# Zero rows behind each expert's last row: eight plain stores on SyncE in place of sixteen indirect scatters on GpSimd

## The chip, the cores and the metric

The kernel runs on one core of one Trainium2 chip. The metric is device time in microseconds (us). Of the kernel before, three runs are shown: 447.7, 451.47 and 451.76 us, median 451.47 us. Times inside the text are those of one profiled execution, counted from the start of its span.

## What is computed

A retention layer (a linear attention with a decaying state) over 4 batches, 8 heads, 768 steps and head size 64 gives 3072 token rows of 512 numbers. Those rows go through a mixture of 8 experts, of which each token takes one:

```python
logits = x @ w_gate + modality_bias[modality_id]
e_idx = np.argmax(logits, axis=1)
...
for e in range(E):
    mask = e_idx == e
    ...
    h = np.maximum(x[mask] @ w1[e], 0.0)          # 512 x 1024
    out[mask] = gate_w[mask, None] * (h @ w2[e])  # 1024 x 512
```

## The kernel before, in words

**Rows on the way.** Token rows are made 128 at a time (24 chunks, three of them a group). As soon as a group's experts are known, `scatter` (L410) writes its rows with indirect DMAs on POOL into a DRAM tensor, `x_dram`, that has room for 3072 rows for each expert; a row's place is its expert's base plus its rank in that expert. A row is 514 numbers (2056 bytes): 512 values, the token's number, the gate.

**Jobs.** The expert work is cut into jobs of one slot each: 256 rows of one expert. There are ten jobs "e", two after each of five groups (`EVENTS`), which take slots that are already full, and two jobs "s" at the end, which take the largest of what is left. Counted from 0, the e jobs are 0 to 9, the s jobs 10 and 11. What is left over goes in units of 32 rows (`unit`, two of them written out, the rest in a loop at the end). A unit or an s job can read past an expert's last row; rows of zeros with token number 3072, which the final scatter drops, must stand there.

**A job on the engines** (`run_job`, 16 steps t = 0 to 15). Steps 0 to 7 are `first_slot` (`h_e`, L763), steps 8 to 15 `second` (`o_e`, L778), all in fp32 pieces. PE's order is the order of the code. In job k the next job's inputs are fetched: at t = 2 SP issues four loads of the first weights (`raw`, L703, skipped when the expert is the same as the job's before), at t = 8 `rows_in` issues two loads of 128 rows each from `x_dram` (`xg_e`, `load_rows`, L729) and then the second weights, and at t = 12 `flip_x` puts eight transposes of those rows into PE's stream (`xp_e`, L748), in the middle of job k's own `o_e` matmuls. Places and experts come from lists in SBUF; SP reads each number into a register (`TENSOR_LOAD`, `reg`, L873).

**The queue of SP** is in the code's order too. SP holds one DMA until its waits are met, and everything behind it holds with it. Its DMAs count on eight semaphores in turn, DMAHW0 to DMAHW7, and each first waits for the last DMA on its own semaphore.

**The rows of zeros before.** Behind the last group's routing, `route` puts pieces into a list `todo` that one tick at every odd step works off: `final_m`, `final_b` (which writes the list `lst_f`, L689), `pad_a`, `pad_b`, and then eight times `pad_c`. These fall into job 7 and after. `pad_a` counts the rows of each expert (a matmul into `tot`, L424) and works out on DVE, over all partitions, two places for each partition and expert; `pad_b` ends that, and `pad_c(e)` issues two indirect DMAs on POOL (L470) that write a tile of zeros `zer2` to rows behind expert e's last one up to the slot's end. Places out of range are dropped. All sixteen are in the group `x_rows` with the scatters and the e jobs' row loads: no member of it waits for another. In POOL's queue they stand among the indirect stores of results (`out_dram`, L791), whose row numbers lie in the tiles `xg`.

Of the kernel before, what the change touches and what calls it, by code (L numbers as in the profile page):

```python
# [7 lines left out]
F32 = mybir.dt.float32  # L8
F32R = mybir.dt.float32r
BF16 = mybir.dt.bfloat16  # L10
I32 = mybir.dt.int32
AF = mybir.ActivationFunctionType
ALU = mybir.AluOpType
AX = mybir.AxisListType

P = 128
# [9 lines left out]
NCAND = NE * SPE  # L26
NSLOT = NT // SLOT


EVENTS = {1: -1, 2: 1, 4: -1, 5: 1, 6: -1}  # L30
NEV = 2
# [3 lines left out]
NTAIL = 2  # L35
NUNIT = 144
DENSE = 9
EMPTY = 2 * NCAND
ZROW = NE * NT

ROW = DM + 2
XW = P + 2 * NE
# [8 lines left out]
def kernel(  # L51
# [94 lines left out]
    def setup_b(modi):  # L146
        nc.vector.tensor_tensor(upper, mask, ident, op=ALU.subtract)
        modf = cp.tile([P, NN], F32, name="modf")
        nc.vector.tensor_copy(modf, modi[:, :, 0])
        modn = cp.tile([P, NN], F32, name="modn")  # L150
        nc.vector.tensor_scalar(modn, modf, -1.0, 1.0, op0=ALU.mult, op1=ALU.add)
        tb2 = wk.tile([P, NN, NE], F32, tag="xs", name="tb2", bufs=6)
        full = [P, NN, NE]
        nc.vector.tensor_tensor(
            tbias, modf.unsqueeze(2).to_broadcast(full), mb[:, 1:2, :].to_broadcast(full),
            op=ALU.mult,
        )
        nc.vector.tensor_tensor(
            tb2, modn.unsqueeze(2).to_broadcast(full), mb[:, 0:1, :].to_broadcast(full),
            op=ALU.mult,  # L160
        )
        nc.vector.tensor_tensor(tbias, tbias, tb2, op=ALU.add)
        nc.vector.tensor_copy(iota3, iota_e.unsqueeze(1).to_broadcast([P, GRP, NE]))
        nc.vector.tensor_scalar(iota3m, iota3, float(NE), None, op0=ALU.subtract)
        nc.vector.tensor_scalar(ebase, iota3, float(NT), None, op0=ALU.mult)

    def zero_rows(nm):
        zer = wk.tile([P, ROW], F32, tag="xs", name=nm, bufs=6)
# [253 lines left out]
    def pad_a():  # L422
        tot = bank("tot")[:, :NE]
        nc.tensor.matmul(tot, ones, cnt[NGRP], start=True, stop=True)  # L424
        shape = [P, NE, 2]
        at = cp.tile(shape, F32, name="pad_at")
        row = cp.tile([P, 2], F32, name="pad_row")
        nc.gpsimd.iota(
            row, [[P, 2]], base=0, channel_multiplier=1, allow_small_or_imprecise_dtypes=True
        )  # L430

        num = cp.tile([P, NE], F32, name="pad_num")
        nc.vector.tensor_copy(num, tot)
        numi = cp.tile([P, NE], I32, name="pad_numi")
        nc.vector.tensor_copy(numi, num)
        lasti = cp.tile([P, NE], I32, name="pad_lasti")
        nc.vector.tensor_scalar(lasti, numi, SLOT - 1, None, op0=ALU.bitwise_and)
        last = cp.tile([P, NE], F32, name="pad_last")
        nc.vector.tensor_copy(last, lasti)
        none = cp.tile([P, NE], F32, name="pad_none")  # L440
        nc.vector.tensor_scalar(none, last, 0.0, float(SLOT), op0=ALU.is_equal, op1=ALU.mult)
        nc.vector.tensor_tensor(last, last, none, op=ALU.add)
        nc.vector.tensor_tensor(
            at, last.unsqueeze(2).to_broadcast(shape), row.unsqueeze(1).to_broadcast(shape),
            op=ALU.add,
        )
        over = cp.tile(shape, F32, name="pad_over")
        nc.vector.tensor_scalar(
            over, at, float(SLOT), float(2 * ZROW), op0=ALU.is_ge, op1=ALU.mult
        )  # L450
        nc.vector.scalar_tensor_tensor(
            num, iota3[:, 0], float(NT), num, op0=ALU.mult, op1=ALU.add
        )
        mid["pad"] = (row, num, over)

    def pad_b():
        row, num, over = mid.pop("pad")
        shape = [P, NE, 2]
        nc.vector.tensor_tensor(
            over, over, num.unsqueeze(2).to_broadcast(shape), op=ALU.add  # L460
        )
        mid["zero"] = zero_rows("zer2")
        pad = mid["pad"] = cp.tile(shape, I32, name="pad_i")
        nc.vector.tensor_tensor(
            pad, over, row.unsqueeze(1).to_broadcast(shape), op=ALU.add
        )

    def pad_c(e):
        for h in range(2):
            ins = nc.gpsimd.indirect_dma_start(  # L470
                out=x_dram[:, :],
                out_offset=bass.IndirectOffsetOnAxis(ap=mid["pad"][:, e, h : h + 1], axis=0),
                in_=mid["zero"],
                in_offset=None,
                bounds_check=ZROW - 1,
                oob_is_err=False,
            )
            disjoint(ins, "x_rows")


    off_c = cnd[:, 0:1]
# [15 lines left out]
    def list_consts():  # L497
        ord_r = small("ord_r", [NCAND, U])
        nc.gpsimd.iota(
            ord_r, [[1, U]], base=0, channel_multiplier=0,  # L500
            allow_small_or_imprecise_dtypes=True,
        )

        vals = small("vals", [NCAND, 4], BF16)
        for i in range(2):
            nc.vector.tensor_scalar(
                vals[:, i : i + 1], id_c, 2.0, float(i - EMPTY), op0=ALU.mult, op1=ALU.add
            )
        nc.vector.tensor_copy(vals[:, 2:3], ex_c)
        pick = small("pick", [NCAND, NE])  # L510
        nc.vector.tensor_scalar(pick, iota_e[:NCAND], ex_c, None, op0=ALU.is_equal)

        nc.vector.tensor_scalar(
            vals[:, 3:4], id_c, float(UPS), float(-UPS * NCAND), op0=ALU.mult, op1=ALU.add
        )
        nc.vector.tensor_reduce(
            sel, ident.rearrange("p (j t) -> p t j", t=UNIT), axis=AX.X, op=ALU.add
        )

        same = small("same", [NCAND, NCAND], BF16)  # L520
        nc.vector.tensor_copy(
            same.rearrange("p (e i) -> p e i", i=SPE),
            pick.unsqueeze(2).to_broadcast([NCAND, NE, SPE]),
        )
        lc["same"] = same
        onef = small("onef", [NCAND, NCAND])
        nc.gpsimd.memset(onef, 1.0)
        keep = small("keep", [NCAND, 1])
        nc.vector.memset(keep, 1.0)
        base_e = small("base_e", [1, 3 * NEV])  # L530
        nc.gpsimd.memset(base_e[:, : 2 * NEV], float(EMPTY))
        nc.gpsimd.memset(base_e[:, 2 * NEV :], 0.0)
        n = 3 * NFIN
        base_f = small("base_f", [1, n + 2 * U + 1])
        nc.gpsimd.memset(base_f, 0.0)
        nc.gpsimd.memset(base_f[:, : 2 * NFIN], float(EMPTY))
        nc.gpsimd.memset(base_f[:, n : n + U], float(NCAND * UPS))
        lc.update(ord_r=ord_r, vals=vals, onef=onef, base_e=base_e, base_f=base_f)
        mid["keep"] = keep

# [413 lines left out]
    def route(gr):  # L954
# [31 lines left out]
        def wait():  # L986
            pass

        if gr == min(EVENTS):

            a()
            todo.extend([a1, lambda: [b(), c()], d])
        elif gr == 0:
            todo.extend([lambda: [a(), a1()], b, c, guess_b])
        elif gr < 5:
            todo.extend([a, a1, b, c])
            if gr in EVENTS:
                todo.append(d)
        else:

            todo.extend([a, a1, wait, b, wait, c])
            if gr in EVENTS:
                todo.extend([wait, d])
            if last:
                todo.extend([wait, final_m, wait, final_b, pad_a, wait, pad_b, wait])
                todo.extend([lambda e=e: pad_c(e) for e in range(NE)])

    def retention(modi):
        quarters(-1)
# [35 lines left out]
    def everything():  # L1045
# [38 lines left out]
        for k in range(len(jobs)):  # L1084
            for t, _ in enumerate(run_job(k)):
                if t % 2:
                    tick()
                if t % 3 == 1:
                    next(ret, None)
                if (k, t) in steps:  # L1090
                    u = steps[k, t]
                    if u not in units:
                        at = 3 * NFIN + u
                        lst = lists["final"]
                        units[u] = unit(
                            f"u{u}", reg(lst, at + U, NE - 1), reg(lst, at, NCAND * UPS)
                        )
                    next(units[u], None)
        assert next(ret, None) is None and not todo
# [7 lines left out]
    with tc.For_i(NTAIL, nun, 1) as iv:  # L1107
        e = nc.values_load(
            lst[0:1, bass.ds(iv + (at + U), 1)], engines=[SP], min_val=0, max_val=NE - 1
        )  # L1110
        cd = nc.values_load(
            lst[0:1, bass.ds(iv + at, 1)], engines=[SP], min_val=0, max_val=NCAND * UPS
        )
        for _ in unit("dyn", e, cd):
            pass


def _layout(inputs):
# [29 lines left out]
    ci = np.arange(NCAND)  # L1148
    cand = np.zeros((NCAND, 4), f)
    cand[:, 0] = (ci % SPE) * SLOT  # L1150
    cand[:, 1] = ci
    cand[:, 2] = ci // SPE

    mod = np.asarray(inputs["moe_modality_id"]).astype(np.int64).reshape(NN, P)
# [54 lines left out]
```

## Time and profile before

| | |
|---|---|
| median of three runs | 451.47 us |
| the profiled execution | 451.09 us, span 449.1 us, mean clock 0.965 |
| PE busy | 402.3 us (90%) |
| DVE / ACT / POOL busy | 245.6 / 208.5 / 106.4 us |
| DMA moved | 92.83 MB, mean 207 GB/s |
| indirect DMAs of zero rows | 16, issued from 322.6 to 348.0 us |
| job 7 on PE | first `h_e` at 307.65 us, transposes for job 8 at 326.84 us |

How to read it: the span runs from the first to the last instruction; what the profiled execution takes beyond it (2.0 us) lies around it. A busy PE says little by itself, since matmuls overlap; whether PE waits is read from gaps in its timeline and from the rows of who waited for whom. POOL's indirect DMAs count as busy time for the making of descriptors, not for the transfer. "SPq" rows are what SP's queue did.

### The profile page before, as it was taken

How to read it: one execution, taken by the hardware profiler on the slowest of the kernel's cores; microseconds unless marked ns; L12 is line 12 of the kernel's file. 1: busy time of each engine (PE TensorE's matmuls, PEld its weight loads, DVE VectorE, ACT ScalarE, POOL GpSimd, SP SyncE). 2: the span in 40 equal slices, each digit the busy share in tenths (PEclk: the TensorE clock that was granted, in tenths of full speed). 3: DMA queues.
4: the chain of work that ended last, by engine and by line, in shares of the span. 5: the costliest groups of instructions: out<-in, count | busy, mean ns of one | idle time of the engine just before them, and what ended most of it. 6: DMA issues, size and time to landing. Idle time of an engine off the chain costs nothing.

```text
span 449.1 us, 13145 instructions
## 1 busy us (share of the span) xinstructions
PE 402.3 (90%) x5160; PEld 353.8 (79%) x5160; DVE 245.6 (55%) x584; ACT 208.5 (46%) x419; POOL 106.4 (24%) x130
## 2 busy tenths in 40 slices
PE   3677679799999999899989899999999999999990
PEld 3566569677988997897988898989999898878860
DVE  1256536576574656465664675687655573725500
ACT  1333335444745644554456455645464654536310
POOL 2324302023214112602231104030287201001010
PEclk9989967899999999899999999999999999999996
DMA  8992867964579784423783205673162899995000
GB/s 291 390 391 84 311 233 257 290 227 123 193 250 358 255 311 165 143 74 117 281 242 137 74 1 159 207 240 98 23 209 103 294 365 343 406 384 195 2 24 19
DMA packets 30895, 92.83 MB, mean 207 GB/s; under 512 B 5550, under 2 KB 5678, under 8 KB 30832
## 3 DMA queue, kind: packets, MB, share of 16 engines
q1 hardware_dynamic: 25360, 77.83, 50.3%
q0 software_dynamic: 5184, 13.67, 7.9%
q8 instruction: 41, 0.67, 0.6%
q10 hardware_dynamic: 288, 0.48, 0.3%
q14 instruction: 22, 0.18, 0.1%
HBM read 94.81 MB, written 17.21 MB: 249 GB/s over the span
## 4 chain that ended last, share of the span: by engine, by line
PE 53%; issue 29%; DMA 5%; POOL 5%; DVE 3%; ACT 2%; POOLq 0%; ACTq 0%; SPq 0%
PE h_e L763 19%; PE o_e L778 16%; PE x L304 5%; PE st L263 5%; PE y L263 4%; PE sc L263 4%; DMA x_dram<-xs,pos 2%; POOL out_dram L791 2%; POOL x_dram L470 2%; DMA cst<-in_consts_dram 1%; PE xp_e L748 1%; ACT hi_e L707 1%; DVE lo_e L709 1%; DMA xg_e<-x_dram 1%; DMA out_dram<-o_e,xg_e 1%
## 5 line engine op out<-in xcount | busy, mean ns | idle before, releaser
L709 DVE TENSOR_TENSOR lo_e<-raw,hi_e 128x1024 fp32r<-128x1024 f32 x80 | 100.4, 1255 | 73.3 <-ACT hi_e L707 69.3
L763 PE MATMUL h_e<-xTh,hi_e 128*128 128x256 f32 x320 | 93.3, 292 | 0.0
L763 PE MATMUL h_e<-xTh,lo_e 128*128 128x256 f32 x320 | 91.3, 285 | 0.0
L763 PE MATMUL h_e<-xTl,hi_e 128*128 128x256 f32 x320 | 91.2, 285 | 0.0
L707 ACT CAST hi_e<-raw 128x1024 fp32r<-128x1024 f32 x80 | 83.9, 1048 | 0.0
L778 PE MATMUL o_e<-hi_e,hTh 128*128 128x512 f32 x160 | 66.3, 415 | 0.0
L778 PE MATMUL o_e<-lo_e,hTh 128*128 128x512 f32 x160 | 63.2, 395 | 0.0
L778 PE MATMUL o_e<-hi_e,hTl 128*128 128x512 f32 x160 | 63.0, 394 | 0.0
L763 PEld LDWEIGHTS h_e<-xTh,hi_e 128*128 128x128 f32 x320 | 62.1, 194 | 1.0
L763 PEld LDWEIGHTS h_e<-xTh,lo_e 128*128 128x128 f32 x320 | 62.0, 194 | 0.3
L763 PEld LDWEIGHTS h_e<-xTl,hi_e 128*128 128x128 f32 x320 | 61.9, 193 | 0.0
L942 POOL TENSOR_TENSOR vd<-kv,cst 128x512 f32<-128x512 f32 x24 | 27.6, 1150 | 116.4 <-DMA kv<-in_qkv_dram 92.6
L326 ACT ACTIVATE xs<-x,cst 128x64 f32<-128x64 f32 x96 | 22.3, 315 | 54.3 <-issue 41.2
L717 DVE SCALAR_TENSOR_TENSOR hTl<-h_e,hTh 128x256 fp32r<-128x256 f32 x80 | 33.1, 420 | 26.1 <-ACT hTh L716 25.9
L716 ACT ACTIVATE hTh<-h_e 128x256 fp32r<-128x256 f32 x80 | 30.5, 390 | 32.0 <-PE h_e L763 27.0
L263 PE MATMUL st<-vd,kv 64*64 64x64 f32 x704 | 34.8, 243 | 9.4 <-issue 6.5
L410 POOL DMA_INDIRECT x_dram<-xs,pos x24 | 26.5, 1105 | 69.5 <-DVE lh L312 30.9
L258 ACT COPY s<-st 128x256 f32<-128x256 f32 x44 | 16.4, 373 | 57.1 <-PE y L263 29.4
L791 POOL DMA_INDIRECT out_dram<-o_e,xg_e x20 | 23.4, 1170 | 77.1 <-ACT o_e L790 75.6
L263 PEld LDWEIGHTS st<-vd,kv 64*64 64x64 f32 x704 | 28.9, 153 | 15.3 <-issue 10.9
L263 PE MATMUL sc<-kq 64*64 64x64 f32 x768 | 33.2, 236 | 8.6 <-DMA kq<-in_qkv_dram 5.4
L263 PE MATMUL y<-kq,s 64*64 64x64 f32 x704 | 31.6, 237 | 6.9 <-issue 6.9
(179 smaller groups left out, 710.9 us busy)
## 6 DMA issues: line engine op xcount, KB each, us to landing
raw<-in_w_dram SPq DMA_DIRECT2D x104, 512.0 KB
kv<-in_qkv_dram SPq DMA_DIRECT2D x24, 512.0 KB
kq<-in_qkv_dram SPq DMA_DIRECT2D x23, 512.0 KB
xg_e<-x_dram SPq DMA_DIRECT2D x20, 257.0 KB
wa_u<-in_w_dram SPq DMA_DIRECT2D x8, 512.0 KB
wb_u<-in_w_dram SPq DMA_DIRECT2D x16, 256.0 KB
xg_s<-x_dram SPq DMA_DIRECT2D x4, 257.0 KB
x_dram<-xs,pos POOLq DMA_INDIRECT x24
```

The costliest lines, as they stand in the source:

```text
L263: nc.tensor.matmul(out_, l, r, start=start, stop=True, skip_group_check=True)
L304: nc.tensor.matmul(px[:, g], yT[:, 2 * u + g], wgt[:, 2 * u + g], start=(g == 0), stop=(g == 1), skip_group_check=True,)
L326: nc.scalar.activation(x[:, i], px[:, i // 2, rows(i % 2)], AF.Copy, scale=gain[:, c, 4 * u + i : 4 * u + i + 1],)
L410: ins = nc.gpsimd.indirect_dma_start(out=x_dram[:, :], out_offset=bass.IndirectOffsetOnAxis(ap=pos[:, i : i + 1], axis=0), in_=xs, in_offs ...
L707: nc.scalar.copy(hi, raws[m][i])
L709: nc.vector.tensor_tensor(lo, raws[m][i], hi.bitcast(F32), op=ALU.subtract)
L716: nc.scalar.activation(hi, src, AF.Relu)
L717: nc.vector.scalar_tensor_tensor(lo, src, 0.0, hi.bitcast(F32), op0=ALU.max, op1=ALU.subtract)
L763: nc.tensor.matmul(ph, s["w1"][f // 2][wi][:, o : o + P], s["xT"][kc // 2][a][:, kc % 2, :], start=(n == 0), stop=(n == 3 * KC - 1),)
L778: nc.tensor.matmul(po, hT[f][a][:, hh * P : (hh + 1) * P], s["w2"][f // 2][wi][:, (f % 2) * DM : (f % 2 + 1) * DM], start=(n == 0), stop=( ...
L791: ins = nc.gpsimd.indirect_dma_start(out=out[:, :], out_offset=bass.IndirectOffsetOnAxis(ap=xg.bitcast(I32)[:, DM : DM + 1], axis=0), in_= ...
L942: ins = nc.gpsimd.tensor_tensor(vds[n], vv, dec[:, n % NCH].unsqueeze(2).to_broadcast([P, H, D]), op=ALU.mult)
```

## The change

Each expert's room in `x_dram` grows from 12 to 13 slots (`SPP`), so that a store of 256 whole rows behind the last row stays inside it. Constants that hold places follow that. `pad_a` is now one DVE operation that gives a list of eight places, one for each expert, on one partition. `pad_b` reads the eight into SP's registers and issues eight plain DMAs on SP, each of 256 rows of zeros (526,336 bytes) from the same tile of 128 rows. They are declared free of dependence on the scatters, one by one; they are not put into the group `x_rows`. `pad_c` is gone.

```diff
+SPP = SPE + 1
+PLACE = SPP * SLOT
...
-ZROW = NE * NT
+ZROW = NE * PLACE
...
     def pad_a():
         tot = bank("tot")[:, :NE]
         nc.tensor.matmul(tot, ones, cnt[NGRP], start=True, stop=True)
-        shape = [P, NE, 2]
-        at = cp.tile(shape, F32, name="pad_at")
-        row = cp.tile([P, 2], F32, name="pad_row")
...
+        lst = mid["pad"] = cp.tile([1, NE], I32, name="pad_at")
         nc.vector.scalar_tensor_tensor(
-            num, iota3[:, 0], float(NT), num, op0=ALU.mult, op1=ALU.add
-        )
-        mid["pad"] = (row, num, over)
...
-    def pad_c(e):
-        for h in range(2):
-            ins = nc.gpsimd.indirect_dma_start(
-                out=x_dram[:, :],
-                out_offset=bass.IndirectOffsetOnAxis(ap=mid["pad"][:, e, h : h + 1], axis=0),
-                in_=mid["zero"],
...
+            lst, iota3[0:1, 0], float(PLACE), tot[0:1], op0=ALU.mult, op1=ALU.add
+        )
+
+    def pad_b(at):
+        zero = zero_rows("zer2")
+        for r in at:
+            ins = nc.sync.dma_start(
+                x_dram[bass.ds(r, SLOT), :].rearrange("(h p) r -> p h r", p=P),
+                zero.unsqueeze(1).to_broadcast([P, 2, ROW]),
             )
-            disjoint(ins, "x_rows")
+            i = getattr(ins, "ins", ins)
+            for to in sum(scattered.values(), []):
+                tc.declare_no_dep(i, to, reason="rows of no token")
...
+        def pads():
+            pad_b([reg(mid["pad"], e, ZROW - SLOT) for e in range(NE)])
...
-                todo.extend([wait, final_m, wait, final_b, pad_a, wait, pad_b, wait])
-                todo.extend([lambda e=e: pad_c(e) for e in range(NE)])
+                todo.extend([wait, final_m, wait, final_b, pad_a, wait, pads])
```

**SP's queue at the end of job 8's first weights, before** (`raw` are weight tiles, `xg_e` the rows of job 8; a row ends with the semaphores it waits for, DMASW being POOL's DMAs):

```order
L703 DMA raw_105<-in_w_dram 128x1024 [waits DMAHW2_49,DVE_49]
L729 ISA
L729 DMA xg_e_5310<-x_dram 128x514 [waits DMAHW3_49,DMASW4_49,PE_49]
L729 ISA
L729 DMA xg_e_5312<-x_dram 128x514 [waits DMAHW4_49,DMASW5_49,PE_49]
```

The same place now (`pad_at` is the list of places, `zer` the tile of zeros):

```order
L667 DMA raw_105<-in_w_dram 128x1024 [waits DMAHW2_49,DVE_49]
L1072 TENSOR_LOAD lst_f [waits DVE_49]
L1072 ISA x2
L837 TENSOR_LOAD pad_at [waits DVE_49]
...
L436 DMA x_dram<-zer_5361 128x2x514 [waits DMAHW3_49,Pool_49]
L436 ISA
L436 DMA x_dram<-zer_5361 128x2x514 [waits DMAHW4_49,DMAHW3_49]
...
L436 DMA x_dram<-zer_5361 128x2x514 [waits DMAHW2_49,DMAHW1_49]
L693 ISA
L693 DMA xg_e_5379<-x_dram 128x514 [waits DMAHW2_49,DMASW4_49,PE_49]
```

Nine register loads and eight stores now stand ahead of job 8's rows. The stores count on DMAHW3, 4, 5, 6, 7, 0, 1 and 2; from the second on, each also waits for the full count of the store before it, and job 8's first row load waits for DMAHW2, the last store. The register load of `lst_f` at the head stood behind job 8's rows and two of its second weights before.

**POOL's queue from the end of job 6's results, before:**

```order
L791 DMA out_dram<-o_e_5071,xg_e_4547 3072x512
L470 DMA x_dram<-zer_5298,pad_i 24704x514 x6
L791 DMA out_dram<-o_e_5340,xg_e_4939 3072x512
L470 DMA x_dram<-zer_5298,pad_i 24704x514 x7
L791 DMA out_dram<-o_e_5408,xg_e_4941 3072x512
L470 DMA x_dram<-zer_5298,pad_i 24704x514 x3
L791 DMA out_dram<-o_e_5676,xg_e_5310 3072x512
```

And now:

```order
L755 DMA out_dram<-o_e_5071,xg_e_4547 3072x512
L755 DMA out_dram<-o_e_5409,xg_e_4939 3072x512
L755 DMA out_dram<-o_e_5465,xg_e_4941 3072x512
L755 DMA out_dram<-o_e_5697,xg_e_5379 3072x512
L755 DMA out_dram<-o_e_5753,xg_e_5381 3072x512
```

The result stores of job 7 (the second and third row of the latter) no longer stand behind six and thirteen scatters of zeros. PE's and ACT's orders are the same in both kernels; on DVE ten small operations of `pad_a` and `pad_b` are gone.

More of the change, by code (lines that the diff above doesn't have):

```diff
@@ L37 @@
 DENSE = 9
-EMPTY = 2 * NCAND
-ZROW = NE * NT
+EMPTY = 2 * NE * SPP
+ZROW = NE * PLACE
 ROW = DM + 2
@@ L164, in setup_b @@
         nc.vector.tensor_scalar(iota3m, iota3, float(NE), None, op0=ALU.subtract)
-        nc.vector.tensor_scalar(ebase, iota3, float(NT), None, op0=ALU.mult)
+        nc.vector.tensor_scalar(ebase, iota3, float(PLACE), None, op0=ALU.mult)
     def zero_rows(nm):
@@ L424, in pad_a @@
         nc.tensor.matmul(tot, ones, cnt[NGRP], start=True, stop=True)
-        shape = [P, NE, 2]
-        at = cp.tile(shape, F32, name="pad_at")
-        row = cp.tile([P, 2], F32, name="pad_row")
-        nc.gpsimd.iota(
-            row, [[P, 2]], base=0, channel_multiplier=1, allow_small_or_imprecise_dtypes=True
-        )
[L432 to L445, printed above, removed]
-        )
@@ L447, in pad_a @@
[L447 to L451, printed above, removed]
-            num, iota3[:, 0], float(NT), num, op0=ALU.mult, op1=ALU.add
-        )
-        mid["pad"] = (row, num, over)
[L456 to L466, printed above, removed]
@@ L468, in pad_c @@
-    def pad_c(e):
-        for h in range(2):
-            ins = nc.gpsimd.indirect_dma_start(
-                out=x_dram[:, :],
-                out_offset=bass.IndirectOffsetOnAxis(ap=mid["pad"][:, e, h : h + 1], axis=0),
-                in_=mid["zero"],
-                in_offset=None,
-                bounds_check=ZROW - 1,
-                oob_is_err=False,
-            )
-            disjoint(ins, "x_rows")
+        lst = mid["pad"] = cp.tile([1, NE], I32, name="pad_at")
+        nc.vector.scalar_tensor_tensor(
+            lst, iota3[0:1, 0], float(PLACE), tot[0:1], op0=ALU.mult, op1=ALU.add
+        )
@@ L513, in list_consts @@
         nc.vector.tensor_scalar(
-            vals[:, 3:4], id_c, float(UPS), float(-UPS * NCAND), op0=ALU.mult, op1=ALU.add
+            vals[:, 3:4], id_c, float(UPS), float(-UPS * NE * SPP), op0=ALU.mult, op1=ALU.add
         )
@@ L536, in list_consts @@
         nc.gpsimd.memset(base_f[:, : 2 * NFIN], float(EMPTY))
-        nc.gpsimd.memset(base_f[:, n : n + U], float(NCAND * UPS))
+        nc.gpsimd.memset(base_f[:, n : n + U], float(NE * SPP * UPS))
         lc.update(ord_r=ord_r, vals=vals, onef=onef, base_e=base_e, base_f=base_f)
@@ L1095, in everything @@
                         units[u] = unit(
-                            f"u{u}", reg(lst, at + U, NE - 1), reg(lst, at, NCAND * UPS)
+                            f"u{u}", reg(lst, at + U, NE - 1), reg(lst, at, NE * SPP * UPS)
                         )
@@ L1111 @@
         cd = nc.values_load(
-            lst[0:1, bass.ds(iv + at, 1)], engines=[SP], min_val=0, max_val=NCAND * UPS
+            lst[0:1, bass.ds(iv + at, 1)], engines=[SP], min_val=0, max_val=NE * SPP * UPS
         )
@@ L1150, in _layout @@
     cand[:, 0] = (ci % SPE) * SLOT
-    cand[:, 1] = ci
+    cand[:, 1] = ci // SPE * SPP + ci % SPE
     cand[:, 2] = ci // SPE
```

## The prediction

> **What bounds the kernel now.** I read the page's head and chain first, then the stages around the change, then single rows.
>
> ```profile
> span 449.1 us, 13145 instructions
> PE 402.3 (90%) x5160; PEld 353.8 (79%) x5160; DVE 245.6 (55%) x584; ACT 208.5 (46%) x419; POOL 106.4 (24%) x130
> PE 53%; issue 29%; DMA 5%; POOL 5%; DVE 3%; ACT 2%; POOLq 0%; ACTq 0%; SPq 0%
> ```
>
> PE sets the time. The chain of waits gives 5% to POOL, the indirect scatters of zeros among it, which suggests a gain; but a chain that ends in a store on POOL follows POOL's queue back, and does not say that PE waited. So I looked at PE in the stretch in which the scatters run (the columns are PE, PEld, DVE, ACT, POOL busy, granted clock, DMA share, GB/s):
>
> ```profile
> L470 POOL DMA_INDIRECT x_dram<-zer,pad_i x16: 977/982/2025, 322.6 to 348.0; - x16
> 316.00:320.00 4.00, 4.00 (x35) 4.00 (x34) 3.32 (x12) 2.78 (x5) 0.00 (x0) 1.00 0.00 0
> 324.00:328.00 4.00, 4.00 (x23) 3.35 (x23) 0.64 (x1) 2.15 (x4) 2.95 (x4) 1.00 0.81 245
> 344.00:348.00 4.00, 4.00 (x19) 3.08 (x17) 2.30 (x4) 1.96 (x5) 3.09 (x4) 1.00 0.17 66
> 348.00:352.00 4.00, 3.67 (x20) 2.72 (x20) 1.91 (x4) 2.88 (x5) 1.88 (x2) 1.00 0.68 197
> ```
>
> PE is full at full clock all through, but for 0.33 us near 351. Sixteen scatters that fill POOL for 26 us therefore cost PE almost nothing.
>
> **What the removal gives.** The one dent has this history, from the timelines of POOL, SP and PE and from who waited for whom:
>
> ```profile
> 343.49 1.61 POOL L791 DMA_INDIRECT out_dram<-o_e,xg_e  x1 [0.30 <-issue]
> 347.71 0.94 SPq L729 DMA_DIRECT2D xg_e<-x_dram  x2
> 350.54 0.27 PE L748 MATMUL xp_e<-cst,xg_e 128*128 128x128 f32 x1
> 351.15 0.98 PE L748 MATMUL xp_e<-cst,xg_e 128*128 128x128 f32 x7 [0.34 <-DMA xg_e<-x_dram]
> PEld xp_e L748 <- DMA xg_e<-x_dram: 0.7, 1, 0.7
> ```
>
> A result store of job 7 stood in POOL's queue behind thirteen scatters and went out at 343.5; job 9's rows go into the tile that it reads, so their load went out late, at 347.7, and PE's transposes waited 0.7 us at most. I credit 0.65 us. The ten small DVE operations (0.16 us in the row of `pad_num` below) give nothing: PE was full while they ran.
>
> **What is added, and when it can begin.** The new stores stand on SP ahead of job 8's rows. The rows that time this place, from the timelines of SP, DVE and PE:
>
> ```profile
> 301.57 9.30 SPq L703 DMA_DIRECT2D raw<-in_w_dram  x4
> 311.14 1.25 SPq L729 DMA_DIRECT2D xg_e<-x_dram  x2
> 312.49 0.44 DVE L689 TENSOR_TENSOR lst_f<-ptf,base_f 1x295 int32<-1x295 f32 x1
> 315.58 0.16 DVE L433 COPY pad_num<-tot 128x8 f32<-128x8 f32 x1
> 326.84 0.38 PE L748 MATMUL xp_e<-cst,xg_e 128*128 128x128 f32 x2
> ```
>
> SP is through job 8's first weights at 310.9 and loaded its rows at 311.1, 15 us ahead of PE's use at 326.84. Now it stops there for `lst_f` (ready at 312.9) and then for the list of places, which DVE writes where it wrote `pad_num`: ready about 315.8. PE makes `tot` ahead of the stall, so nothing moves that earlier. Then come eight register loads. Two such loads in a row, from SP's own instructions:
>
> ```profile
> L873 SPq TENSOR_LOAD <-lst x2: 263/264/264, 321.9 to 322.5; - x2
> L873 SPq FUSED_REGOPS  x2: 147/150/152, 322.2 to 322.8; - x2
> ```
>
> One each 0.6 us: 8 x 0.6 = 4.8 us, begun at 316.0, so the first store goes out at about 320.9 (with 0.1 us of register work).
>
> **What one store costs.** If eight stores could be in flight together, SP would pay eight issues. They cannot: each waits for the last one's full count, since all write the same tensor at places that only registers know. So one store's time from issue to count is paid eight times, in SP's queue. No row of before shows a plain store of 526,336 bytes. The nearest are a pair of row loads, which together move just that, in rows of the same length, and two indirect stores of half as much:
>
> ```profile
> 64.08 0.34 SPq L729
> 64.63 2.86 DMA xg_e<-x_dram
> 67.53 1.75 PE xp_e L748 x7
> 64.00:66.00 2.00, 0.02 (x1) 0.00 (x0) 0.51 (x3) 0.93 (x4) 1.04 (x1) 0.98 0.48 112
> 66.00:68.00 2.00, 0.94 (x3) 0.65 (x4) 0.00 (x0) 0.00 (x0) 0.00 (x0) 0.50 0.40 151
> 332.08 2.86 DMA out_dram<-o_e,xg_e
> 337.65 1.95 DMA x_dram<-zer,pad_i
> 52.00:54.00 2.00, 1.15 (x38) 0.75 (x28) 0.21 (x1) 0.02 (x1) 1.69 (x2) 1.00 1.04 418
> ```
>
> The pair: first issue at 64.08, both landed at 67.49, 3.4 us; (112 + 151) x 2 us = 526 KB, so nothing else was moving. The second issue trails the first by 0.5 us, which one DMA would not, so 3.3 us. An indirect store of 262 KB took 2.86 us, POOL's 0.98 us of descriptors among it; another 263 KB at the pair's 151 GB/s would add 1.7 us and SP's issue (0.34) would take the place of POOL's: 4.0 us. I take 3.3 us, by the pair, since its bytes and rows are the same and it is SP's own path; 0.15 us of waking and register work makes 3.45 us for each. Bounds: below, a scatter of zeros, of which some rows are dropped, with the missing 263 KB at the peak of 418 GB/s: 1.95 + 0.63 = 2.6 us; above, the indirect store with the missing bytes at 151 GB/s and nothing taken off: 2.86 + 1.7 = 4.6 us.
>
> **The sum.** 8 x 3.45 = 27.6 us: the last store lands at 348.5. Job 8's rows wait for it, then need 0.2 us of register work and the pair's 3.4 us: 352.1. PE wants them at 326.84 and, its order being fixed, has no other work: a stall of 25.3 us. With 2.6 and 4.6 us a store (2.75 and 4.75 with the 0.15): 22.0 and 38.0 us, stalls of 19.7 and 35.7 us.
>
> What is queued behind on SP: job 8's second weights and job 9's first. SP's own instructions show the former skipped:
>
> ```profile
> L703 SPq DMA_DIRECT2D raw<-in_w_dram x96: 73/333/841, 65.4 to 393.1; - x96
> L703 SPq DMA_DIRECT2D raw<-in_w_dram x1: 84/84/84, 312.8 to 312.8; - x1
> ```
>
> That issue took 84 ns where the median is 333 ns, and the latter are used by job 8's steps 9 to 15, which move back with the stall; nothing else becomes late. The result stores on POOL are freed. Behind the stall PE runs on at its old pace, but not at once:
>
> ```profile
> 68.00:70.00 2.00, 2.00 (x35) 1.67 (x37) 0.75 (x2) 1.26 (x3) 0.00 (x0) 0.50 0.26 63
> 70.00:72.00 2.00, 2.00 (x88) 2.00 (x84) 1.75 (x2) 1.13 (x2) 0.00 (x0) 0.50 1.06 387
> 72.00:74.00 2.00, 2.00 (x46) 1.91 (x39) 0.78 (x2) 1.01 (x3) 1.04 (x1) 0.82 0.90 285
> ```
>
> After the idle time of 64 to 67.5 PE had a granted clock of 0.50 until about 72.7. Lost there: 0.47 x 0.5 + 2 x 0.5 + 2 x 0.5 + 2 x 0.18 = 2.6 us. I take 2.4 us (1.6 to 3.0, since part of the return came out of lighter work). The Trainium skill, page "TensorE: Matmul & The Clock Gate", Part 1, says that an idle window of some 3.4 us drops the array to half rate and a busy one of 3.4 us gives it back; by that the loss is estimated at 1.7 us and the sum would be 0.7 us less. The rows show a return in 5 us here, so they decide.
>
> 451.09 + 25.3 + 2.4 - 0.65 = 478.1; against the median of 451.47 that is 26.6 us more, 5.9%. **Predicted: 478 us.** Low end of this case: 451.09 + 19.7 + 1.6 - 0.65 = 471.7; high end: 451.09 + 35.7 + 3.0 - 0.65 = 489.1.
>
> **Rivals.**
>
> *The stores overlap.* If the waits between them were met early, SP would issue one each 0.5 us and the transfers would run at the peak: 4.21 MB at 418 GB/s is 10.1 us, the last landing near 320.9 + 10.1 + 2 = 333.0 (2 us of latency from the small scatter's 1.95). Rows at 336.6, stall 9.8 us, time 451.09 + 9.8 + 2.4 - 0.65 = 462.6. For it: between 316 and 320 the DMA engines are empty (share 0.00). Against it: the order of the instructions names a wait on the last store at every store. 10%.
>
> *Not slower: PE never waits and POOL's relief is all.* If job 8's rows did not have to wait for the stores, or the last store landed by 326.84 - 3.6 = 323.2, the point from which this decides, the stores would be free and the 0.65 us stay: 450.4. For it: sixteen POOL issues of 0.98 us give way to eight SP issues of some 0.35 us (`xg_e`'s was 0.34), and the result stores no longer queue behind zeros. Against it: bytes alone need 10.1 us from 320.9, and the load's row names the last store's semaphore. 4%. The Trainium skill's page "DMA: Bandwidth & Descriptors", section "Issuing engine by pattern", speaks for this case: simple stores belong on SyncE, which it calls generally faster than GpSimd's path. No run here sets the two paths against each other for one store.
>
> *Each store is much slower.* A transfer can take far longer than the pair:
>
> ```profile
> 54.62 9.44 DMA x_dram<-xs,pos
> ```
>
> That scatter met DMA engines full of loads (418 GB/s just before it, above). Here SP itself is stopped, so no loads compete; but a store to DRAM could carry a tail of its own. At 6 us: 8 x 6.15 = 49.2, rows at 373.9, stall 47.1, time 451.09 + 47.1 + 2.4 - 0.65 = 499.9. 6%.
>
> **How the numbers follow.** Forecast 80%, overlap 10%, not slower 4%, much slower 6%. The forecast's own range is 472 to 489; a range that also takes in the overlap case leaves out 10% and some tails: 461 to 489. A measurement of this kernel tells about 1% (4.5 us) from no change. Slower by over 1%: the forecast, the overlap and the slow case, 96%; within 1%: 3%; faster by over 1%: 1%, the tail of the not-slower case.
>
> **What would show it.** Right: on SP eight stores 3 to 4.6 us apart from about 321, then two row loads near 349; PE idle from about 327 to 352, ended by `xg_e`; a granted clock of 0.5 for some 4 us behind it; POOL free of zeros; job 9's transposes without a wait; nothing else longer. The steps fall one by one if: the first store is not near 321 (register loads); the stores lie 0.5 us apart (waits between them); PE's gap is there but ends on another tile (order of SP). The whole forecast is wrong if PE shows no gap of more than 5 us in job 7.

## The result, and the profile after

| | before | after |
|---|---|---|
| median | 451.62 us (6 runs) | 474.69 us (5 runs) |
| ratio, 95% interval | | 1.0514 (1.0459 to 1.057) |
| profiled execution / span | 451.09 / 449.1 us | 472.25 / 470.5 us |
| mean clock | 0.965 | 0.947 |

The change makes the kernel slower by 5.1%, 20.7 to 25.7 us. (A sixth run of after, at 662 us, had a mean clock of 0.561 against 0.934 to 0.947 in the others and is left out.) The head of the page after, with its rows of slices for PE and for the granted clock, 11.8 us a slice:

```profile
span 470.5 us, 13150 instructions
PE 402.5 (86%) x5160; PEld 353.5 (75%) x5160; DVE 243.3 (52%) x574; ACT 208.1 (44%) x419; POOL 87.5 (19%) x113
PE   4668787989999998999999999994049999999991
PEclk9998789889999999999999999999559999999997
```

PE has the same busy time as before (402.5 against 402.3 us) in a span that is 21.4 us longer. The slices say where: 28 to 30, about 318 to 353 us, read 4, 0 and 4. The chain of waits between 300 and 380 us now goes through that hole (first the shares of this stretch, then start, length, what):

```profile
by line: DMA x_dram<-zer 34.9%; issue 29.4%; PE o_e L742 7.3%; PE h_e L727 5.6%; SPq L837 4.3%; DMA raw<-in_w_dram 4.0%; POOL out_dram L755 3.7%; DMA xg_e<-x_dram 3.5%; DVE lo_e L673 3.1%; PE xp_e L712 2.2%; ACT hi_e L671 1.3%; SPq L693 0.7
...
312.04 0.07 DVE pad_at L429
...
316.85 3.20 DMA x_dram<-zer
320.07 3.35 DMA x_dram<-zer
323.44 3.52 DMA x_dram<-zer
326.97 3.83 DMA x_dram<-zer
330.82 3.50 DMA x_dram<-zer
334.44 3.50 DMA x_dram<-zer
337.95 3.48 DMA x_dram<-zer
341.45 3.51 DMA x_dram<-zer
345.08 0.38 SPq L693
345.71 2.79 DMA xg_e<-x_dram
348.54 1.75 PE xp_e L712 x7
```

The eight stores follow one another with at most 0.12 us in between, 28.1 us from the first issue (316.85) to the last landing (344.96); job 8's rows come behind the last one, and PE starts when they are there. PE's own timeline, and the list of who waited for whom between 310 and 380 us (total, times, longest), say the same:

```profile
347.94 2.35 PE L712 MATMUL xp_e<-cst,xg_e 128*128 128x128 f32 x8 [24.57 <-DMA xg_e<-x_dram]
373.73 1.03 PE L712 MATMUL xp_e<-cst,xg_e 128*128 128x128 f32 x8
```

```profile
PEld xp_e L712 <- DMA xg_e<-x_dram: 25.4, 2, 25.0
PE xp_e L712 <- DMA xg_e<-x_dram: 24.6, 1, 24.6
```

The windows of the stall and of the return (columns as in the prediction):

```profile
334.00:338.00 4.00, 0.00 (x0) 0.00 (x0) 0.00 (x0) 0.00 (x0) 0.00 (x0) 0.50 0.35 132
350.00:352.00 2.00, 2.00 (x7) 1.61 (x6) 1.49 (x3) 1.59 (x3) 0.00 (x0) 0.50 0.46 115
352.00:354.00 2.00, 2.00 (x10) 1.60 (x9) 1.12 (x1) 0.00 (x0) 0.00 (x0) 0.94 0.98 387
```

Between 334 and 338 every engine is idle and the DMA engines carry 132 GB/s at a third of their share. That points to latency and not to bandwidth; the run with half of each store, below, tests it.

**A measure that does not depend on the chip.** Kernels that were run on different chips start the stage at different times. So I compare the time from `tot` (the count of rows, ahead of everything that the change moves) to the last `uf_u` (PE's last work for the left-over units). The two rows, before and after:

```profile
314.00 0.18 PE L424 MATMUL tot<-cnt,ones 128*128 128x8 bf16 x1
432.77 1.04 PE L858 MATMUL uf_u<-uos_u,sel 128*32 128x512 f32 x2
```

```profile
310.37 0.18 PE L427 MATMUL tot<-cnt,ones 128*128 128x8 bf16 x1
455.40 1.05 PE L822 MATMUL uf_u<-uos_u,sel 128*32 128x512 f32 x2
```

118.77 us before, 145.03 us after: +26.26 us. Below this is called the stage.

### The profile page after: what moved, and what is told of

The parts are those of the page before. It is cut to its first block, busy times and chain, and to the rows that moved or that the text cites. A ratio compares the mean times of both kernels' runs of the same rounds, so it can differ in the third digit from the quotient of the medians.

```text
span 470.5 us, 13150 instructions
## 1 busy us (share of the span) xinstructions
PE 402.5 (86%) x5160; PEld 353.5 (75%) x5160; DVE 243.3 (52%) x574; ACT 208.1 (44%) x419; POOL 87.5 (19%) x113
## 4 chain that ended last, share of the span: by engine, by line
PE 51%; issue 27%; DMA 11%; DVE 3%; POOL 3%; ACT 2%; SPq 1%; POOLq 0%; ACTq 0%
PE h_e L727 18%; PE o_e L742 16%; DMA x_dram<-zer 6%; PE x L307 5%; PE st L266 4%; PE y L266 3%; PE sc L266 3%; POOL out_dram L755 2%; DMA x_dram<-xs,pos 2%; PE xp_e L712 2%; DVE lo_e L673 1%; ACT hi_e L671 1%; DMA cst<-in_consts_dram 1%; DMA xg_e<-x_dram 1%; SPq L837 1%
## 5 line engine op out<-in xcount | busy, mean ns | idle before, releaser
L742 PE MATMUL o_e<-hi_e,hTh 128*128 128x512 f32 x160 | 67.4, 421 | 0.0
L906 POOL TENSOR_TENSOR vd<-kv,cst 128x512 f32<-128x512 f32 x24 | 28.1, 1170 | 113.3 <-DMA kv<-in_qkv_dram 78.3
L680 ACT ACTIVATE hTh<-h_e 128x256 fp32r<-128x256 f32 x80 | 30.5, 389 | 26.8 <-PE h_e L727 23.4
L266 PE MATMUL st<-vd,kv 64*64 64x64 f32 x704 | 33.4, 236 | 9.5 <-issue 6.6
L266 PEld LDWEIGHTS st<-vd,kv 64*64 64x64 f32 x704 | 27.5, 146 | 15.1 <-issue 10.7
L266 PE MATMUL y<-kq,s 64*64 64x64 f32 x704 | 30.0, 229 | 8.2 <-issue 8.2
```

The lines of the kernel that those rows point to most:

```text
L266: nc.tensor.matmul(out_, l, r, start=start, stop=True, skip_group_check=True)
L680: nc.scalar.activation(hi, src, AF.Relu)
L742: nc.tensor.matmul(po, hT[f][a][:, hh * P : (hh + 1) * P], s["w2"][f // 2][wi][:, (f % 2) * DM : (f % 2 + 1) * DM], start=(n == 0), stop=( ...
L906: ins = nc.gpsimd.tensor_tensor(vds[n], vv, dec[:, n % NCH].unsqueeze(2).to_broadcast([P, H, D]), op=ALU.mult)
```

## Experiments

The theory: each store waits for the last one's full count, so eight latencies of 3.5 us stand in SP's queue ahead of job 8's rows, and PE waits for these. The rivals: the stores' bytes set the time; SP or the DMA engines are simply slow with such a store; the new layout of `x_dram`, rather than the stores, costs something; or the rows' wait alone, not SP's held queue, does it. The kernels of the first group ran on one chip (before: 450.67 us there), those of the second on another (before: 444.81), those of the third on a third (before: 444.62). Where one execution alone was timed, no ratio is given, and the stage is what counts.

### The layout alone

The kernel before with 13 slots of room for each expert, and nothing else changed:

```diff
+SPP = SPE + 1
+PLACE = SPP * SLOT
...
-ZROW = NE * NT
+ZROW = NE * PLACE
...
-        nc.vector.tensor_scalar(ebase, iota3, float(NT), None, op0=ALU.mult)
+        nc.vector.tensor_scalar(ebase, iota3, float(PLACE), None, op0=ALU.mult)
...
```

> The kernel before with one part of the change alone: 13 slots of room for each expert instead of 12; the sixteen indirect scatters stay. The changed kernel's profile stood 3.6 us earlier than before's already at the count of rows (tot), ahead of any moved instruction. Theory (that is spread between runs): ratio 0.995 to 1.005 to the kernel before. Rival (the new places spread the early scatters better): ratio 0.992 or less, and the first transposes of job 0 near 64.6 us, not 66.8.

Measured: 451.76 us, ratio 1.0001 (0.996 to 1.0043); stage 118.69 us. The layout costs nothing that shows.

### The same stores from POOL's queue, with the waits between them

```diff
-            ins = nc.sync.dma_start(
+            ins = nc.gpsimd.dma_start(
...
-            pad_b([reg(mid["pad"], e, ZROW - SLOT) for e in range(NE)])
+            pad_b([reg(mid["pad"], e, ZROW - SLOT, ET.Pool) for e in range(NE)])
```

> The eight plain stores on POOL with all waits kept: each for the last one, job 8's rows for the eighth. SP is not held by them, only its row load waits. Theory (the chain): stores 3.5 to 4.2 us apart, gap in PE 24 to 33 us, time 474 to 484 us. Rival (SP's queue, held and so late with all its loads, is what costs): gap under 10 us. A store on POOL is expected 0.3 to 0.7 us longer than on SP.

Measured in one execution: 479.54 us; stage 150.71 us (+31.94). The timeline of POOL, whose brackets hold the idle time ahead and what ended it; the timeline of SP; and PE's wait:

```profile
318.56 0.76 POOL L436 DMA_DIRECT2D x_dram<-zer  x1 [11.71 <-DVE hTl L681]
322.77 0.75 POOL L436 DMA_DIRECT2D x_dram<-zer  x1 [3.45 <-DMA x_dram<-zer]
...
347.26 0.71 POOL L436 DMA_DIRECT2D x_dram<-zer  x1 [3.22 <-DMA x_dram<-zer]
```

```profile
351.53 0.96 SPq L693 DMA_DIRECT2D xg_e<-x_dram  x2
```

```profile
PE xp_e L712 <- DMA xg_e<-x_dram: 30.5, 2, 30.3
```

Here SP is not held by the stores themselves, and it is worse: each of POOL's stores is released by the one before it, 4.1 us apart (28.70 us over seven steps, in one of which a store of results comes between), and the rows still wait for the last. So the chain of eight does the harm to job 8's rows, on whichever queue it stands.

### The stores from POOL, without waits between them

Each store is declared free of dependence on the other seven, as it writes the rows behind another expert. Job 8's rows still wait for all of them.

```diff
             for to in sum(scattered.values(), []):
                 tc.declare_no_dep(i, to, reason="rows of no token")
+            for to in padded:
+                tc.declare_no_dep(i, to, reason="rows of other experts")
+            padded.append(i)
```

> The eight plain stores on POOL, free of each other, but job 8's rows still wait for the last. Theory: stores 1.3 to 1.6 us apart, bytes overlap, gap in PE at job 8's transposes 6 to 12 us, time 457 to 464 us. Rival (the stores' bytes, not the waits between them, make the 28 us): gap 20 us or more.

Measured in one execution: 465.29 us; stage 133.93 us (+15.16). POOL's and SP's timelines, three windows of 2 us, and PE's wait:

```profile
321.23 5.75 POOL L437 DMA_DIRECT2D x_dram<-zer  x8 [11.70 <-DVE lo_e L677]
```

```profile
336.57 0.95 SPq L697 DMA_DIRECT2D xg_e<-x_dram  x2
```

```profile
324.00:326.00 2.00, 2.00 (x10) 1.65 (x9) 0.00 (x0) 0.58 (x1) 2.00 (x4) 1.00 0.99 356
330.00:332.00 2.00, 0.00 (x0) 0.00 (x0) 0.00 (x0) 0.00 (x0) 0.00 (x0) 0.96 1.02 323
332.00:334.00 2.00, 0.00 (x0) 0.00 (x0) 0.00 (x0) 0.00 (x0) 0.00 (x0) 0.50 1.04 385
```

```profile
PE xp_e L716 <- DMA xg_e<-x_dram: 12.6, 1, 12.6
```

POOL hands over all eight in 5.75 us, one each 0.72 us (half of the 1.3 to 1.6 us expected), the DMA engines are full (share about 1.0), and the gap falls from 30.5 to 12.6 us. What is left is mostly bytes: 4.21 MB at 323 to 385 GB/s between 324 and 334 us. The gap and the time are a little above the 6 to 12 us and the 457 to 464 us expected, since I had reckoned with a faster rate.

### The stores from POOL, and the rows free of them too

The e jobs read only slots that are full of tokens, so their loads need not wait for any row of zeros:

```diff
+                for to in padded:
+                    tc.declare_no_dep(i, to, reason="rows of other slots")
```

> The eight plain stores issued on POOL, with the registers read there, free of each other and with the e jobs' row loads free of them. Theory (the stall is the chain of eight store latencies ahead of job 8's rows): no gap over 1 us in PE at the transposes of jobs 8 and 9, time 449 to 452 us, ratio 0.995 to 1.001. Rival (plain stores of 4.2 MB cost by their bytes or by contention wherever they stand): a gap or slower matmuls, 455 us or more.

Measured: 446.46 us, ratio 0.9919 (0.9884 to 0.9954); stage 118.05 us (-0.72). POOL's and SP's timelines:

```profile
318.65 5.75 POOL L437 DMA_DIRECT2D x_dram<-zer  x8 [11.70 <-DVE lo_e L677]
```

```profile
339.67 1.26 SPq L697 DMA_DIRECT2D xg_e<-x_dram  x2
```

The same stores now cost PE nothing that shows, and this kernel is faster than before by 0.8% (0.5% to 1.2%) and than the changed one. Job 9's rows go out at 339.67, 7.8 us ahead of PE's use at 347.49, and none of PE's transposes in this stretch waits. The 0.72 us of the stage are as expected, but the whole gain (2.1 to 5.2 us) is larger, and the time below the 449 to 452 us expected; the rest lies outside the stage, and the last group of experiments comes back to it.

### Half of each store

```diff
-                x_dram[bass.ds(r, SLOT), :].rearrange("(h p) r -> p h r", p=P),
-                zero.unsqueeze(1).to_broadcast([P, 2, ROW]),
+                x_dram[bass.ds(r, P), :],
+                zero,
```

> The changed kernel with stores of 128 rows instead of 256, half the bytes (the second 128 rows behind each expert's last row are left out). Measured so far: 3.5 us a store of 526 KB, DMA engines busy a third of it. Theory (latency, not bytes): 2.7 to 3.0 us a store, gap in PE 18 to 21 us. Rival (bytes): 1.8 us a store, gap 11 us.

Measured in one execution: 464.13 us; stage 139.60 us (+20.83). SP's own instructions (min, median and longest ns; first and last issue), and PE's wait:

```profile
L436 SPq DMA_DIRECT2D x_dram<-zer x8: 332/333/369, 314.2 to 334.3; - x8
```

```profile
PE xp_e L712 <- DMA xg_e<-x_dram: 19.4, 2, 19.2
```

Seven steps in 20.1 us are 2.87 us for each store of 263 KB, against 3.51 us for 526 KB. Half the bytes take off only 0.64 us, which is 411 GB/s; a line through the two sizes leaves 2.23 us whatever the size. It is a rough line, since single steps lie between 2.57 and 3.15 us and between 3.22 and 3.85 us. If bytes set the time, a step would have halved.

The Trainium skill, page "DMA: Bandwidth & Descriptors", section "Anatomy of one DMA — SWDGE (gpsimd) path", fits a fixed 2.0 us and bytes over 436 GB/s for GpSimd's path; by that two stores of these sizes are estimated at 3.2 and 2.6 us. SP's stores here show the same shape at 0.3 us more; POOL's own, above, took 4.0 us a step for the larger size, 0.8 us more than the estimate.

### Every store twice

```diff
-        for r in at:
+        for r in at + at:
```

> The changed kernel with each of the eight stores issued twice, sixteen in a row. Theory: each link of the chain costs 3.5 us on PE, gap 51 to 54 us, time 500 to 504 us. Rival (a cost that comes once, as SP's stop or the cold clock): gap under 35 us.

Measured in one execution: 494.13 us; stage 172.68 us (+53.91).

```profile
L436 SPq DMA_DIRECT2D x_dram<-zer x16: 372/372/428, 311.0 to 363.0; - x16
```

```profile
PE xp_e L712 <- DMA xg_e<-x_dram: 52.0, 2, 51.8
```

Fifteen steps in 52.0 us are 3.47 us each, and the gap grows by 27.4 us for eight more stores. The cost goes by the number of stores, each at its full latency. (The bound for the whole time, 500 us and more, had been reckoned from the first chip; this one is some 6 us faster.)

### The stores one tick later, behind job 8's rows

```diff
-                todo.extend([wait, final_m, wait, final_b, pad_a, wait, pads])
+                todo.extend([wait, final_m, wait, final_b, pad_a, wait, wait, pads])
```

> The changed kernel with the eight stores one tick later, at step 9 of job 7 instead of 7, so that they stand behind job 8's rows and second weights in SP's queue. Theory: job 8's transposes do not wait; SP is held from about 325 to 355 (in the time of before) and job 9's first weights and rows are late: a gap of 8 to 18 us in job 8, time 460 to 471 us. Rival (the stores cost only by the rows that wait for them directly): no gap over 3 us in job 7 or 8, 450 to 454 us.

Measured in one execution: 457.63 us; stage 134.47 us (+15.70). SP's timeline and PE's wait:

```profile
318.86 25.68 SPq L436 DMA_DIRECT2D x_dram<-zer  x8
347.23 2.49 SPq L667 DMA_DIRECT2D raw<-in_w_dram  x4
350.00 0.92 SPq L693 DMA_DIRECT2D xg_e<-x_dram  x2
```

```profile
PE xp_e L712 <- DMA xg_e<-x_dram: 13.8, 2, 13.7
```

Job 8's transposes (at 319.15) wait for nothing now. The stall moves to job 9, whose rows go out at 350.00 behind the stores and behind its weights, and is shorter, as PE has had job 8's work to do meanwhile. The last store, issued at 344.17, had landed at 347.56, so at 350.00 these rows waited for no store any more but had only now their turn in SP's queue, behind register loads and four weights that the stores had held up. So a held queue does the harm too: the same chain makes PE wait 24.6 or 13.8 us by what stands behind it. (The 457.63 us are below the 460 to 471 expected, which had also been reckoned from the first chip.)

### Four stores behind job 8's rows, four behind job 9's

```diff
...
-                todo.extend([wait, final_m, wait, final_b, pad_a, wait, pads])
+                todo.extend([wait, final_m, wait, final_b, pad_a, wait, wait, lambda: pads(0)])
+                todo.extend([wait] * 7 + [lambda: pads(1)])
```

> The changed kernel with four stores at step 9 of job 7 and four at step 9 of job 8, each half behind the rows of the next job in SP's queue. Theory: half the chain (14 us and four register loads) fits between two row loads; gaps in PE of 0 to 4 us in all, time 451 to 457 us. Rival (four stores already hold up the weights of the s jobs and units, for which the DMA engines are full from 356 to 405 in before): 458 to 468 us.

Measured: 444.52 us, ratio 0.9991 (0.9955 to 1.0027); stage 122.51 us (+3.74).

```profile
314.64 11.16 SPq L436 DMA_DIRECT2D x_dram<-zer  x4
...
331.54 0.96 SPq L693 DMA_DIRECT2D xg_e<-x_dram  x2
...
339.87 14.31 SPq L436 DMA_DIRECT2D x_dram<-zer  x4
...
360.33 1.03 SPq L693 DMA_DIRECT2D xg_s<-x_dram  x2
```

```profile
PE xp_s L712 <- DMA xg_s<-x_dram: 2.5, 2, 2.1
```

With all waits kept, still on SP, 25 us of held queue in two pieces cost 2.5 us of PE at the s jobs. The rest of the stage's +3.74 us is mostly the clock, whose granted share is 0.66 from 368 to 370 us and 0.50 from 370 to 372. The gap is as expected; the time is below the 451 to 457 us, again reckoned from the first chip. The harm is the piece that is longer than the slack of the load behind it.

The eight stores on SP without waits between them were not run, so that what SP's queue alone would cost with them is not shown.

### What gives the rest of POOL's gain?

With the free stores on POOL the stage explains 0.72 us of a gain of 2.1 to 5.2 us. In that profile `tot` came at 311.12 us, against 314.00 in the profile before. One suspect was the `iota` into `pad_row`, which the change drops and which POOL does early in the program. It is held back here in the kernel before, and added to the free stores of POOL in a second kernel; the free stores alone run beside them:

```diff
         row = cp.tile([P, 2], F32, name="pad_row")
-        nc.gpsimd.iota(
+        with tc.issue_after(vd_last[0]):
+            nc.gpsimd.iota(
...
```

> The kernel before with one instruction moved: the iota that makes pad_row, which POOL ran at 11.5 us between two memsets, now runs behind the last decay of v (near the end of the retention). Kernels without that early iota stood 2 to 4 us earlier at the count of rows than before and layout, though nothing else differs ahead of it. Theory (the early iota on POOL shifts the first stage): ratio 0.990 to 0.995. Rival (spread between runs, or where tiles lie): ratio 0.997 to 1.003.

> The kernel with eight free plain stores on POOL, with the early iota of pad_row put back (its tile is then not used). Theory of the early iota: the 0.8% gain falls to the 0.65 us predicted for the freed rows of job 9, ratio 0.997 to 1.000. Rival: ratio stays at 0.989 to 0.995.

> The kernel with eight free plain stores on POOL once more, on the same chip as the two with the iota moved. Theory and rival alike: ratio 0.988 to 0.995; if it comes out at 0.997 to 1.000, the 0.8% of its first measurement was chance.

Measured: 444.19 us, ratio 0.9978 (0.9951 to 1.0004), with the late `iota`; 442.26 us, 0.9955 (0.9929 to 0.9981), with the free stores and the early `iota`; 442.83 us, 0.9949 (0.9923 to 0.9974), with the free stores alone. The `iota` is not it: with it or without it the free stores are 0.5% faster (the 0.9955 lies between the two ranges set for it, next to the rival's). The stage of the last is 118.05 us, as on the first chip. The gain of the last is 1.2 to 3.4 us. Of it 0.7 lie in the stage and about 0.2 behind the last `uf_u` (16.1 us left there, against 16.3 in before). Another 0.3 lie outside the span: in every run of the free stores the device time is 1.6 to 1.7 us longer than the span, in every run of before 2.0 to 2.1. Where the rest comes from, up to 2.2 us, stays open. Single profiles do not settle it: on the first chip `tot` came at 314.45 us with the layout alone, but with the stores on POOL at 311.12 (free), 311.01 (all waits) and 313.70 (no waits between them).

One thing more came of this. The kernel with the late `iota` keeps all sixteen scatters and yet has a stage of 118.06 us: its load of job 9's rows went out at 343.92 us, 3.5 us ahead of PE's use, and was just in time, where the kernel before had 2.8 us and was 0.6 us late. Of POOL's four issues from 338.93 to 343.49 us in before, two took 1.69 and 1.61 us (1.64 and 1.57 in the layout kernel, where PE waits the same 0.3 us); here the same four took 0.98 to 1.21 us. The relief that I credited is thus a near miss. Each kernel was profiled once, so whether the moved `iota` or chance made the difference is not shown.

## Why the prediction was right, point by point

The forecast case came: 478 us against 474.69 measured, and a stall of the length and in the place that were named. Its terms, all in the two profiles:

| step | predicted | measured |
|---|---|---|
| list of places to first store | about 5.1 us | 4.8 us (312.09 to 316.85) |
| eight stores, issue to last landing | 27.6 us | 28.1 us (3.51 each) |
| last landing to PE's start | 3.6 us | 3.0 us (344.96 to 347.94) |
| stall of PE | 25.3 us | 24.7 us |
| lost to the low clock | 2.4 us | 2.1 us |
| relief of job 9's rows | -0.65 us | -0.56 us |
| sum, in the stage | 27.05 us | 26.26 us |

**Job 8's stall.** Measured as the time from `tot` to the transposes, 37.57 us against 12.84 (+24.7), or by the bracket of PE's row (24.57). Twice the stores gave 52.0 us, and on POOL the same stores without waits gave 12.6 us where with them they gave 30.5: the waits between the stores make most of the stall, and when job 8's rows did not wait for the stores either, none was left.

**One store.** The pair of row loads (3.3 us, and 0.15 of waking) was the right row to take. By the run with half of each store, it is mostly a fixed latency, which is why a pair of loads, though it moves the other way, could come out the same. Whether its latency is of the same kind was not tried, so that the two agree within 0.1 us may be partly luck.

**The clock.** From job 8's transposes to job 9's took 25.79 us (347.94 to 373.73) where it was 23.70 before: 2.1 us. The granted clock is 0.50 up to 352 and 0.94 between 352 and 354, full from about 352.2, so 4.3 us after PE's start. In the runs with all waits on POOL, without waits between, with half stores and with double stores the same distance is 25.73 to 26.66 us, 2.0 to 3.0 us more than before: this term varies by 1 us from run to run.

The Trainium skill's page "TensorE: Matmul & The Clock Gate", Part 1, has 3.4 us for that, by which the loss is estimated at 1.7 us; the 4.3 us and 2.1 us of the rows here are more, and they decide.

**The relief** had the right size but a cause that was partly wrong. In the kernel before, the first of job 9's row loads waited for the fourteenth scatter of zeros itself (its semaphore, DMASW5, is that of POOL's scatter at 345.41), and only the second load's tile was held by the result store. Both go when the zeros leave POOL's queue of indirect stores. The kernel with the late `iota` adds that it is a near miss.

**What was mis-sized** lies outside the stage. I set the sum against before's own execution, 451.09 us, and it came out 3.4 us too high against the median; as a difference, 26.6 us were forecast and 20.7 to 25.7 measured. The spans of the two profiled executions add up: 26.26 - 3.63 - 1.23 = 21.4 us.

The 1.23 us lie behind the last `uf_u`, where after has 15.1 us left and before 16.3; the prediction put nothing there. POOL's last long instruction is a closing `DRAIN` (min, median and longest ns), here in before, in after and with the free stores on POOL:

```profile
L1204 POOLq DRAIN  x3: 40/103/5457, 442.8 to 448.8; - x3
L1170 POOLq DRAIN  x3: 40/103/4148, 465.5 to 470.2; - x3
L1176 POOLq DRAIN  x3: 40/109/4812, 439.7 to 445.1; - x3
```

It takes 5457 ns in all three kernels with the sixteen scatters, 4148 ns in all five with the stores on SP and 4812 ns in all five with the stores on POOL. POOL issues 66, 50 and 58 DMAs in these: 0.08 us more for each. So taking sixteen DMAs off POOL gave back 1.3 us at the end. That it is their number, and no other property of these DMAs, was not tested apart.

The 3.63 us are there at `tot`, 2.2 of them by the first transposes (64.62 against 66.79 us). Ahead of these the kernels differ in an `iota` on POOL and in places in `x_dram`, and the kernels with one of these alone showed no difference in time that is clear of noise. By the medians, with 0.2 us that after saves outside the span, some 1.7 us are left for this stretch (26.26 - 1.23 - 0.2 - 23.1), less than the interval of the result is wide; why this execution was early was not found.

**The rivals.** Overlap was priced at 462.6 us; when the waits were taken away, on POOL, it gave 465.29, as the rate was 323 to 385 GB/s and not the peak of 418. "Not slower" was right in naming what frees the stores (rows that need not wait for them) and exists as the free stores on POOL, but not as the change was written. The much slower store did not come; its sum is also 0.2 us off, since 320.9 + 49.2 + 3.6 is 373.7 and not 373.9.

## What to carry to other kernels

Before DMAs are put into a queue in which others stand behind them, ask of each whether it waits for the one before: then the price is their number times the full latency, and halving the bytes saves little. Compare the longest piece of held queue with the slack of the first load behind it; a chain cut in two made PE wait 2.5 us where the whole made it wait 24.6. An engine that looks busy (POOL, 26 us of scatters) can be the cheaper place, as long as PE, which sets the time, does not wait for it.

## What was unexpected in the hardware

- A plain store of 526 KB from POOL, waiting for the last, took 4.0 us a step against 3.5 on SP, and 0.71 to 0.76 us to issue against 0.37. On POOL it was nevertheless the faster kernel, once nothing waited.
- A plain store from SP to DRAM came to about 2.2 us plus its bytes at some 410 GB/s, from two sizes; eight of them in flight together, from POOL, moved 323 to 385 GB/s.
- POOL's closing `DRAIN` was 5457, 4812 and 4148 ns long with 66, 58 and 50 DMAs issued from POOL, some 0.08 us for each, to the nanosecond the same in all profiles of a group.
- Two profiles can be 2.2 us apart by 65 us, far ahead of the stores; a sum of parts is checked better in the stage than by the total.
